# Activation stores of chunks 2 to 5 moved from SyncE's queue to ScalarE's queue in a retention layer followed by a SiLU feed-forward layer

## The chip, the core and the metric

The kernel runs on one core of a Trainium2 chip. The metric is device time in microseconds (us); lower is better. TensorE (PE) multiplies matrices, VectorE (DVE) and ScalarE (ACT) work on tiles element by element, GpSimd (POOL) helps, and SyncE (SP) only issues DMA transfers. In the profile, "PEld" is TensorE's loading of weights, and "SPq" or "ACTq" marks an instruction of an engine's sequencer, such as the issue of a transfer.

## The reference

```python
# q, k, v: (B=4, H=8, S=768, D=64); w_in: (512, 2048); w_out: (2048, 512)
gamma = 1.0 - 2.0 ** (-5.0 - np.arange(H))
for t in range(S):
    state = gamma[None, :, None, None] * state + np.einsum('bhd,bhe->bhde', k[:, :, t], v[:, :, t])
    y[:, :, t] = scale * np.einsum('bhd,bhde->bhe', q[:, :, t], state)
x = y.transpose(0, 2, 1, 3).reshape(B * S, H * D)      # (3072, 512)
h = x @ w_in
g = h * (1.0 / (1.0 + np.exp(-h)))
out = g @ w_out                                        # (3072, 512)
```

The inputs are float32, and every large product is made of three products of split operands.

## The kernel before

**Tiling.** The sequence is cut into NC = 6 chunks of 128 positions. A *unit* is one chunk of one batch, 24 units numbered chunk by chunk. The attention of a unit is spread over three consecutive *visits* (`visit`, `halves`, L606 to L656): transposition of k and q, scores and chunk sums, and then the output y, which is split into three parts `xt` for the next product.

**The first product.** For each chunk c and each of NF = 16 slices f of w_in's columns, `product_in(c, f)` (L659) makes twelve 128x512 matmuls: eight into a PSUM bank `ha` and four into a bank `hb`. Three banks rotate over all ha and hb (`turn`, L376), so a bank is used again by the next product's hb (for an ha) or by the ha of the product after that (for an hb). `close_steps` (L674) then empties them: ACT copies ha to a tile `hs` (L676), DVE subtracts hb (L681), and ACT applies SiLU in place (L686). The result is called g. The pool of `hs` has three buffers (L90).

**The stores in question.** `put_g(keep)` (L689) stores all but the last `keep` of the finished g tiles to a DRAM tile `g_dram` of 256 KB, one per (c, f), by a transfer that SP issues (L692). In the main loop it is called after each product with keep = 1. An `hs` buffer is free again when its store has landed. The name of the last store is kept in `stored`.

**The second product** (`w_out`, `split`, L716 to L737, and the loops from L985 on) starts when all 96 first products are done. It loads the g tiles again (`get`, L698), splits each into three parts on ACT and DVE (L731, L733, L734), and multiplies them with the split w_out. Its outputs are stored by ACT (L1026), but for the last chunk's.

**What sets the order.** PE's order is that of the program. Up to the first visits of chunk 2 the other engines' order is written out by hand too (`early_order`). After that the framework's scheduler orders ACT, DVE, POOL and SP by readiness and program order, within the edges that the kernel draws: `tc.issue_after(x)` puts the instructions of its block behind x on x's own engine, without a wait for x's result.

**SP's other work in the main loop.** From unit 14 on, k and q are transposed by transfers: POOL parts them into 16-bit planes (`part_t`, L415), SP issues two transposing transfers (`turn_t`, L428, issued at L431, whose last is kept in `turned_by`), and ACT joins the planes (`join_t`, L438). SP also loads k, q and v (L164), raw slices of w_in and w_out (`load_w`, L188 for w_out), and stores converted slices (`store_w`, L288). While chunks 3 and 4 are multiplied (`patient`), the raw slices to load are held in `waiting`. In the last six visits the loop (L957 to L968) places SP's work as follows: the two transposes; k and q of the next unit behind them; one product later, v of the next unit behind the latest store of a g; another product later, the waiting raw slices behind the latest store of a g.

During chunk 5's products ACT and DVE also split the w_out slices (L120, L123, L126, L128), which SP loads again (`get_w`, L713).

**Order of the products.** The loop over `steps` runs 92 products: six pairs with chunks 0 and 1, then chunk 2 mixed in for f = 0 to 7, the rest of chunks 0 and 1, chunk 2 for f = 8 to 15, and then chunks 3, 4 and 5. Four products of chunk 0 and 1 come before it. 64 of the 96 products belong to chunks 2 to 5. `LATE` is 2 (L591).

Of the kernel before, what the change touches and what calls it, by code (L numbers as in the profile page):

```python
# [33 lines left out]
def kernel(  # L34
# [28 lines left out]
    nc = tc.nc  # L63
# [17 lines left out]
    def pool(name, bufs, **kw):  # L81
# [14 lines left out]
    g_dram = {(c, f): dram.tile([128, NT], FP32, tag=f"g{c}_{f}", name=f"gd_{c}_{f}")  # L96
              for c in range(NC) for f in range(NF)}
# [48 lines left out]
    def load(name, n):  # L146
        if n >= len(units):
            return
        c, b = units[n]
        src = {"k": k, "q": q, "v": v}[name]  # L150
        if n == 4 * B and name == "k":
            t = conv.tile([128, H, D], FP32, tag="wl", name=f"kf_{n}")
            nc.sync.dma_start(out=t, in_=src[b, :, ds(c * C, C)].rearrange("h t d -> t h d"))
            kqv[name][n] = t
            return
        if n < EARLY:

            if n not in early:
                early[n] = wpool.tile([128, 3, H, D], FP32, tag=f"w{4 + n}", name=f"kqv_{n}")
            t = early[n][:, "kqv".index(name)]  # L160
        else:
            t = ld.tile([128, H, D], FP32, tag=f"{name}f", name=f"{name}f_{n}",
                        bufs=2 if name == "q" else 3)
        nc.sync.dma_start(out=t, in_=src[b, :, ds(c * C, C)].rearrange("h t d -> t h d"))  # L164
        kqv[name][n] = t
# [6 lines left out]
    def load_w(i):  # L172
        if i >= 2 * NF:
            return
        if wide:
            t = stage.tile([128, 2 * DM], U32, tag="wf", name=f"wf_{i}")
            w_in, w_out, n = moe_w_in.bitcast(U32), moe_w_out.bitcast(U32), 256
        else:
            t = stage.tile([128, DM], FP32, tag="wf", name=f"wf_{i}")
            w_in, w_out, n = moe_w_in, moe_w_out, 128  # L180
        if i < NF:
            to = t.rearrange("p (i o f) -> o p i f", o=2, f=n)
            src = w_in[:, ts(i, n)].rearrange("(i o p) f -> o p i f", o=2, p=128)
            nc.sync.dma_start(out=to[0], in_=src[0])
            for j in range(2):
                nc.sync.dma_start(out=to[1, ts(j, D)], in_=src[1, ts(1 - j, D)])
        else:
            nc.sync.dma_start(out=t, in_=w_out[ts(i - NF, 128), :])  # L188
        staged[i] = t
# [71 lines left out]
    def take_w(after=None, parts=False):  # L261

        i = taken[0]
        taken[0] += 1
        if i >= 2 * NF:
            return
        with queue(after) if after else ExitStack():
            rounded = convert_w(i)

        def finish():  # L270
            w32 = rounded()
            if i < NF:
                list(split_w(i, w32, "wi", scale, w_sb))
            else:
                to_store.append((i - NF, w32))

        if parts:
            behind_next.append(finish)
        else:
            with queue(after) if after else ExitStack():  # L280
                finish()
# [3 lines left out]
    def store_w():  # L285
        while to_store:
            f, w32 = to_store.pop(0)
            nc.sync.dma_start(out=wo_dram[f], in_=w32)  # L288
# [101 lines left out]
    def scale_k(n):  # L390
        if 0 <= n < len(units):
            t = kqv["k"][n]
            if units[n][0] == NC - 1:
                t = t[:D]
            if 2 * B + 1 < n < 3 * B + 2:

                def half(heads):
                    for h in heads:
                        nc.scalar.activation(out=t[:, h, :], in_=t[:, h, :], func=AF.Copy,
                                             scale=gk[:, units[n][0], h : h + 1])  # L400

                half(range(H // 2))
                behind_copy.append(lambda: half(range(H // 2, H)))
                return
            g = gk[: t.shape[0], units[n][0], :].unsqueeze(2).to_broadcast([t.shape[0], H, D])
            nc.vector.tensor_tensor(out=t, in0=t, in1=g, op=ALU.mult)
# [6 lines left out]
    planes, turned, turned_by, waiting = {}, {}, [], []  # L413

    def part_t(n, after=None):  # L415

        for name, (p, tag, bufs) in (("q", (ld, "kf", 3)), ("k", (one, "kt", 2))):
            src = kqv[name].pop(n) if name == "q" else kqv[name][n]
            t = p.tile([128, 2 * H * D], U16, tag=tag, name=f"{name}p_{n}", bufs=bufs)
            i = nc.gpsimd.tensor_copy(  # L420
                out=t.rearrange("p (w h d) -> p w h d", w=2, h=H),
                in_=src.bitcast(U16).rearrange("p h (d w) -> p w h d", w=2)).ins
            if after is not None:
                tc.add_manual_dep(i, after.name, mybir.DependencyInfo(
                    mybir.DependencyClass.Sync, mybir.DependencyReason.DATA), reason="later")
            planes[name, n] = t

    def turn_t(n):  # L428
        for name, (p, tag, bufs) in (("q", (ld, "qf", 2)), ("k", (one, "qt", 3))):
            t = p.tile([128, 2 * HP, C], U16, tag=tag, name=f"{name}w_{n}", bufs=bufs)  # L430
            turned_by[:] = [nc.sync.dma_start_transpose(out=t, in_=planes.pop((name, n))).ins]  # L431
            turned[name, n] = t

    def join_t(name, n):

        to, bufs = (qt, 3) if name == "q" else (kt, 2)
        to[n] = one.tile([128, HP, C], FP32, tag=f"{name}t", name=f"{name}t_{n}", bufs=bufs)
        nc.scalar.copy(out=to[n].bitcast(U16).rearrange("p a (t w) -> p w a t", w=2),  # L438
                       in_=turned.pop((name, n)).rearrange("p (w a) t -> p w a t", w=2))
# [151 lines left out]
    LATE = 2  # L591
# [65 lines left out]
    pending, stored = [], []  # L657

    def product_in(c, f):  # L659
        close_in(c, f, *multiply(c, f))  # L660
# [28 lines left out]
    def put_g(keep):  # L689
        while len(pending) > keep:  # L690
            c, f, g = pending.pop(0)
            stored[:] = [nc.sync.dma_start(out=g_dram[c, f], in_=g).ins]  # L692


    order = [(c, f) for c in range(NC) for f in range(NF)]
# [12 lines left out]
    def get_w(f):  # L708
        if f < NF:
            tag = "kqkqq"[f % 5]  # L710
            t = one.tile([128, DM], FP32, tag=f"{tag}t", name=f"wr_{f}",
                         bufs=2 if tag == "k" else 3)
            nc.sync.dma_start(out=t, in_=wo_dram[f])  # L713
            w_got[f] = t

    def w_out(f):  # L716
        list(split_w(f, w_got.pop(f), "wo", 1.0, wo))
        get_w(f + W_READ)
# [117 lines left out]
    SC(4)  # L836
    CL(0), CL(0), CL(0)
    put_g(0)
    W(1)
    T(5)  # L840
# [23 lines left out]
    W(2)  # L864
    CL(1)
    put_g(0)
    T(7)
    P(2)
# [74 lines left out]
    for n, (c, f) in enumerate(steps):  # L943
        if n in scales_at:
            behind_next.append(lambda m=scales_at[n]: scale_k(m))
        if n in joins_at:
            behind_copy.insert(0, lambda m=joins_at[n]: [join_t(name, m) for name in "qk"])
        if n in parts:
            behind_next.append(lambda m=parts[n]: part_t(m, taken_out[0]))
        patient[0] = steps.index((3, 0)) <= n < max(turns_at) + 2  # L950
        product_in(c, f)
        put_g(1)
        store_w()
        if (c, f) in takes:
            take_w(taken_out[0], n < len(pairs + three))
        behind.get((c, f), lambda: None)()
        if n in turns_at:  # L957
            turn_t(turns_at[n])
            if turns_at[n] >= LATER:
                with tc.issue_after(turned_by[0]):  # L960
                    load("k", turns_at[n] + 1), load("q", turns_at[n] + 1)
        if turns_at.get(n - 1, 0) >= LATER:
            with tc.issue_after(stored[0]):
                load("v", turns_at[n - 1] + 1)
        if turns_at.get(n - 2, 0) >= LATER:
            with tc.issue_after(stored[0]):
                while waiting:
                    load_w(waiting.pop(0))  # L968
        for name, m in loads_at.get(n, ()):
            load(name, m)  # L970
        if c == NC - 1:
            if f == 0:
                for i in range(W_READ):
                    get_w(i)
            if f < NF - 4:
                w_out(f)
            if f >= NF - 6:
                if f == NF - 6:
                    for n in range(G_AHEAD):
                        get(n)  # L980
                if f >= NF - S_AHEAD:
                    split(f - NF + S_AHEAD)
# [84 lines left out]
```

## Time and profile before

| What | Value |
|---|---|
| Median of 3 runs (lowest, highest) | 622.12 us (618.11, 622.21) |
| The profiled execution's own time | 620.76 us |
| Its span | 618.9 us, granted TensorE clock 0.999 |
| ACT, SiLU of g (L686) | x96, 627 ns each |
| ACT, copy of ha (L676) | x96, 591 ns each |
| DVE, subtraction of hb (L681) | x96, 683 ns each |
| Stores of g, SP (L692) | x96, 256 KB each, 3.4 us to landing (median) |
| Stores of the output, ACT (L1026) | x20, 256 KB each, 2.1 us to landing (median) |
| Transposing transfers, SP (L431) | x20, 4.2 and 4.5 us to landing (medians) |
| DMA queue q1 (SP's transfers) | 102.79 MB, 59.7% of 16 engines' span |
| DMA queue q10 (ACT's transfers) | 5.24 MB, 2.3% |

The page of a profile gives each engine's busy time and share of the span; a timeline lists instructions by start and duration, with the idle time before one and what ended it in brackets; a list of waits names the waiting line, what it waited for, and total, count and longest in us. The mean of a stage's DMA share is the busy share of the core's 16 DMA engines.

### The profile page before, as it was taken

To read this page: it belongs to the slowest core of one execution; us is meant where nothing else is said; L and a number is where in the kernel's file an instruction comes from. 1 tells how busy PE (TensorE), PEld (TensorE's weight loads), DVE (VectorE), ACT (ScalarE), POOL (GpSimd) and SP (SyncE) were. 2 spreads that over 40 slices of the span, in tenths; PEclk is the share of its full clock that TensorE was granted. 3 is DMA by queue.
4 is the path that set the end of the run, shared out by engine and by line. 5 is a ranking of instruction groups with operands and counts; after the bars stand their busy time and mean duration, and the time that the engine had idled before them with its cause. 6 is when DMAs were issued, how large, how long until landed. Compare 5 with 4: busy or idle time off the path is not lost.

```text
span 618.9 us, 13462 instructions
## 1 busy us (share of the span) xinstructions
PE 601.6 (97%) x5360; PEld 494.6 (80%) x5360; DVE 424.6 (69%) x731; ACT 315.7 (51%) x595; POOL 29.1 (5%) x85
## 2 busy tenths in 40 slices
PE   6898999999999999999999999999999999999997
PEld 5777787888778888887788888888888888888886
DVE  4998889889977777785699783645635453654631
ACT  6677896676667567665588642312221221412311
POOL 3000000100031111120000000000000000000000
PEclk9999999999999999999999999999999999999999
DMA  9998874784789699999777552533524433442301
GB/s 193 221 227 208 220 216 158 202 241 169 250 217 222 184 265 241 275 233 292 273 227 257 193 147 68 169 104 92 180 70 132 140 102 103 141 132 89 116 1 68
DMA packets 144334, 108.88 MB, mean 176 GB/s; under 512 B 101136, under 2 KB 109584, under 8 KB 144272
## 3 DMA queue, kind: packets, MB, share of 16 engines
q1 hardware_dynamic: 141392, 102.79, 59.7%
q10 hardware_dynamic: 2880, 5.24, 2.3%
q8 instruction: 42, 0.69, 0.5%
q14 instruction: 20, 0.16, 0.1%
HBM read 66.06 MB, written 36.70 MB: 166 GB/s over the span
## 4 chain that ended last, share of the span: by engine, by line
PE 73%; DVE 5%; DMA 2%; ACT 2%; issue 1%; SPq 1%; DVEq 0%; POOLq 0%; ACTq 0%
PE o L1007 21%; PE ha L666 18%; PE oa L1007 14%; PE hb L666 10%; PE ob L1007 7%; PE y L513 2%; DMA gd<-g 1%; DVE g L681 1%; DMA yr<-yd 1%; SPq L431 1%; PE sc L474 1%; PE sc L464 1%; DVE ca L218 1%; DVE xt L572 0%; ACT g L676 0%
## 5 line engine op out<-in xcount | busy, mean ns | idle before, releaser
L666 PE MATMUL ha<-xt,wi 128*128 128x512 f32 x768 | 193.7, 394 | 1.3 <-ACT xt L569 0.7
L666 PEld LDWEIGHTS ha<-xt,wi 128*128 128x128 f32 x768 | 141.8, 188 | 33.5 <-ACT xt L569 1.1
L1007 PE MATMUL o<-wo,gs 128*128 128x512 f32 x564 | 143.2, 389 | 0.0
L733 DVE TENSOR_TENSOR gs<-gr,gs 128x512 fp32r<-128x512 f32 x96 | 62.1, 685 | 90.3 <-ACT gs L731 90.3
L1007 PEld LDWEIGHTS o<-wo,gs 128*128 128x128 f32 x564 | 105.9, 188 | 21.9
L731 ACT ACTIVATE gs<-gr 128x512 fp32r<-128x512 f32 x96 | 53.6, 621 | 134.2 <-issue 131.9
L1007 PE MATMUL oa<-wo,gs 128*128 128x512 f32 x376 | 115.8, 389 | 0.0
L666 PE MATMUL hb<-xt,wi 128*128 128x512 f32 x384 | 103.2, 390 | 1.9 <-ACT g L676 0.9
L681 DVE TENSOR_TENSOR g<-g,hb 128x512 f32<-128x512 f32 x96 | 65.6, 683 | 37.1 <-ACT g L676 24.7
L666 PEld LDWEIGHTS hb<-xt,wi 128*128 128x128 f32 x384 | 71.8, 188 | 18.4 <-ACT g L676 1.8
L686 ACT ACTIVATE g<-g 128x512 f32<-128x512 f32 x96 | 60.1, 627 | 46.2 <-DVE g L681 46.2
L1007 PEld LDWEIGHTS oa<-wo,gs 128*128 128x128 f32 x376 | 70.6, 188 | 14.7
L1007 PE MATMUL ob<-wo,gs 128*128 128x512 f32 x188 | 73.7, 392 | 0.0
L676 ACT ACTIVATE g<-ha 128x512 f32<-128x512 f32 x96 | 56.7, 591 | 28.5 <-PE ha L666 11.9
L734 DVE SCALAR_TENSOR_TENSOR gs<-gs 128x512 fp32r<-128x512 f32 x96 | 62.0, 683 | 0.0
L1007 PEld LDWEIGHTS ob<-wo,gs 128*128 128x128 f32 x188 | 35.3, 188 | 8.7 <-DVE o L1025 1.6
L202 ACT ACTIVATE ca<-wf 128x512 f32<-128x512 f32 x32 | 21.4, 668 | 8.0 <-DVE cw L223 5.0
L218 DVE SCALAR_TENSOR_TENSOR ca<-wf,ca 128x512 f32<-128x512 uint32 x32 | 22.7, 710 | 0.5
L1024 ACT ACTIVATE o<-o 128x512 f32<-128x512 f32 x10 | 6.0, 598 | 33.4 <-PE o L1007 33.0
L482 DVE TENSOR_TENSOR am<-sc,decay 128x512 f32<-128x512 f32 x24 | 16.5, 688 | 9.1 <-PE sc L474 9.0
L212 DVE SCALAR_TENSOR_TENSOR cs<-ca,cs 128x512 uint32<-128x512 uint32 x32 | 22.1, 691 | 0.9
L513 PE MATMUL y<-qt,mid 64*64 64x64 f32 x384 | 20.2, 224 | 1.8 <-POOL token L385 1.8
(93 smaller groups left out, 568.4 us busy)
## 6 DMA issues: line engine op xcount, KB each, us to landing
gd<-g SPq DMA_DIRECT2D x96, 256.0 KB, 3.4
gr<-gd SPq DMA_DIRECT2D x96, 256.0 KB, 2.7
wf<-in_moe_w_out_dram SPq DMA_DIRECT2D x16, 512.0 KB, 5.0
out_dram<-o ACTq DMA_DIRECT2D x20, 256.0 KB, 2.1
wf<-in_moe_w_in_dram SPq DMA_DIRECT2D x16, 256.0 KB, 4.2
wf<-in_moe_w_in_dram SPq DMA_DIRECT2D x32, 128.0 KB, 4.0
kf<-in_k_dram SPq DMA_DIRECT2D x16, 256.0 KB, 4.3
qf<-in_q_dram SPq DMA_DIRECT2D x16, 256.0 KB, 4.1
```

Source lines behind the costliest of these rows:

```text
L202: nc.scalar.activation(out=a.bitcast(FP32), in_=hi.bitcast(FP32), func=AF.Abs, scale=65536.0)
L212: nc.vector.scalar_tensor_tensor(out=s, in0=a, scalar=3, in1=s, op0=ALU.logical_shift_left, op1=ALU.bitwise_or)
L218: nc.vector.scalar_tensor_tensor(out=p.bitcast(FP32), in0=lo, scalar=2.0 ** -52, in1=p.bitcast(FP32), op0=ALU.mult, op1=ALU.mult)
L513: i = nc.tensor.matmul(yp[ts(e, D), o, a, :], lhsT=lhsT, rhs=rhs, start=(e, o) not in started, stop=True, skip_group_check=True).ins
L666: nc.tensor.matmul(hb if i == 2 else ha, lhsT=w_sb[f][:, i, ts(kk, 128)], rhs=xt[c][:, i, kk, :], start=kk == 0 and i != 1, stop=kk == KIN ...
L676: copied[:] = [nc.scalar.activation(out=hs, in_=ha, func=AF.Copy, scale=ONE_E).ins]
L681: taken_out[:] = [nc.vector.tensor_tensor(out=hs, in0=hs, in1=hb, op=ALU.subtract).ins]
L686: nc.scalar.activation(out=hs, in_=hs, func=AF.Silu)
L731: nc.scalar.activation(out=t[:, 0, :], in_=g, func=AF.Copy, scale=HALF)
L733: nc.vector.tensor_tensor(out=t[:, 1, :], in0=g, in1=high, op=ALU.subtract)
L734: nc.vector.scalar_tensor_tensor(out=t[:, 2, :], in0=t[:, 1, :].bitcast(FP32), scalar=-1.0 / EPS, in1=high, op0=ALU.mult, op1=ALU.add)
L1007: nc.tensor.matmul(o, lhsT=g, rhs=wo[f][:, i, :], start=f == 0 and i != 1, stop=f == NF - 1 and i != 0)
```

## The change

Stores of g of chunks 2 to 5 (64 of 96) are issued by ACT on its own queue instead of by SP. `stored` is then set only by stores of chunks 0 and 1. The two blocks that put v and the raw slices behind the latest store put them behind the latest transposing transfer instead.

```diff
     def put_g(keep):
         while len(pending) > keep:
             c, f, g = pending.pop(0)
-            stored[:] = [nc.sync.dma_start(out=g_dram[c, f], in_=g).ins]
+            ring = nc.scalar if c >= LATE else nc.sync
+            i = ring.dma_start(out=g_dram[c, f], in_=g).ins
+            if c < LATE:
+                stored[:] = [i]
...
         if turns_at.get(n - 1, 0) >= LATER:
-            with tc.issue_after(stored[0]):
+            with tc.issue_after(turned_by[0]):
                 load("v", turns_at[n - 1] + 1)
         if turns_at.get(n - 2, 0) >= LATER:
-            with tc.issue_after(stored[0]):
+            with tc.issue_after(turned_by[0]):
                 while waiting:
                     load_w(waiting.pop(0))
```

## The prediction

> **What bounds the kernel now.** I read the page first, then busy time by stage, then what TensorE (PE) waited for, then SP's and ACT's instructions around the longest of these waits.
>
> ```profile
> PE 601.6 (97%) x5360; PEld 494.6 (80%) x5360; DVE 424.6 (69%) x731; ACT 315.7 (51%) x595; POOL 29.1 (5%) x85
> ```
>
> PE is busy for 601.6 of 618.9 us, so every stall together is 17.3 us. The change can act only from chunk 2's first product on. Counting steps of 2.72 us (one product, 12 matmuls, in the chain of work) back from the second stage's start at 353.0, and about 2 us for each attention visit, the products of chunk 2 lie at about 110 to 132 us (8 of them) and from 176 us on (56 more, with chunks 3 to 5). Busy time by stage there (columns PE, PEld, DVE, ACT, POOL, clock, DMA share, GB/s):
>
> ```profile
> 98.00:180.00 82.00, 81.16 (x473) 66.10 (x472) 73.22 (x128) 54.94 (x96) 4.59 (x5) 1.00 0.68 208
> 180.00:280.00 100.00, 99.93 (x1456) 82.71 (x1456) 78.07 (x135) 64.91 (x100) 18.24 (x25) 1.00 0.98 238
> 280.00:300.00 20.00, 19.13 (x187) 15.55 (x186) 13.50 (x25) 11.53 (x20) 0.09 (x1) 1.00 0.92 265
> 300.00:320.00 20.00, 19.70 (x146) 16.07 (x145) 15.64 (x28) 14.43 (x26) 0.09 (x1) 1.00 0.78 264
> 320.00:345.00 25.00, 25.00 (x112) 20.49 (x111) 24.84 (x46) 21.02 (x40) 0.00 (x0) 1.00 0.72 245
> ```
>
> PE's idle time is 0.84 + 0.07 + 0.87 + 0.30 = 2.08 us in the whole region: that is the ceiling of any gain, 0.3% of the time. The last row matters for the loss: DVE is at 24.84 of 25 us there, and ACT has 3.98 us to spare. What PE waited for from 176 to 356 us:
>
> ```profile
> PE hb L666 <- ACT g L676: 0.9, 1, 0.9
> PE y L513 <- POOL token L385: 0.3, 1, 0.3
> PE hb L666 <- DVE xt L575: 0.2, 1, 0.2
> ```
>
> Only the first is a matter of stores. Its cause shows on SP and then on ACT:
>
> ```profile
> 278.98 1.28 SPq L431 DMA_TRANSPOSE qw<-qp  x1
> 280.35 2.80 SPq L431 DMA_TRANSPOSE kw<-kp  x1
> 283.25 1.96 SPq L705 DMA_DIRECT2D gr<-gd  x4
> 285.30 0.85 SPq L692 DMA_DIRECT2D gd<-g  x2
> ```
>
> ```profile
> 287.21 0.64 ACT L686 ACTIVATE g<-g 128x512 f32<-128x512 f32 x1
> 292.11 0.60 ACT L676 ACTIVATE g<-ha 128x512 f32<-128x512 f32 x1 [4.26 <-DMA gd<-g]
> ```
>
> A SiLU ended at 281.12, but its store was issued at 285.30, behind two transposing transfers and four loads, and took 6.70 us to land (the chain of work). The three hs buffers were full, the copy out of ha waited 4.26 us, and the bank came free 0.87 us late for PE. The SP queue's own waits show that this is rare and that SP mostly waits for the work:
>
> ```profile
> SPq L692 <- ACT g L686: 48.6, 29, 3.7
> ...
> SPq L692 <- DMA gr<-gd: 1.3, 2, 1.1
> ```
>
> The second line is a store held by an older, unrelated load. That wait would stand on ACT too.
>
> **What the Trainium skill says.** "DMA: Bandwidth & Descriptors", section "Queues, rings and completion order": SP and ACT each own one ring on each of the same 16 DMA engines, without engines or a descriptor generator of their own, and an engine takes turns between the rings packet by packet. So a store on ACT's ring need not follow SP's loads, but shares the engines with them. The trace has SP's rings at 59.7% and ACT's at 2.3%, never both full, so it neither confirms nor denies it. The same page, "Issuing engines are not separate DMA queues": a second issuing engine saves issue time only. With a DMA share of 0.98 from 180 to 280 us I expect the landing (median 4.1 us there) to shorten by less than the queueing. "ScalarE: Activation LUTs", section "What ACT_TABLE_LOAD costs": back-to-back ACTIVATEs overlap by about 93 ns. The trace agrees: 0.62 us activations start 0.52 us apart (323.20, 323.72), an overlap of 0.10, which a store between them forfeits.
>
> **The change part by part.**
>
> *64 stores leave SP* (8 early, 56 after 176 us). SP is not on PE's path except at 292 us. There the store would be issued at about 281.5 instead of 285.3; even 6.7 us of landing then ends before 288.3, and the next stores likewise precede the loads. Gain 0.87 us; between 0 (landing lengthens as much) and 2.08 (everything PE waited for). I take 0.87.
>
> *64 stores join ACT.* The row of an ACT store is 0.338 us of issue (out, x20, at most 0.377). What it costs ACT depends on its place:
>
> ```profile
> 398.03 1.14 ACT L731 ACTIVATE gs<-gr 128x512 fp32r<-128x512 f32 x2
> 398.89 0.34 ACTq L1026 DMA_DIRECT2D out_dram<-o  x1
> 399.27 1.16 ACT L731 ACTIVATE gs<-gr 128x512 fp32r<-128x512 f32 x2
> ```
>
> Here the issue ran while the second activation still did: a third would have begun at 398.03 + 2 x 0.52 = 399.07 and began at 399.27, 0.20 us. A store right behind its own SiLU must wait for its end: 0.63 + 0.02 (semaphore) + 0.34 + about 0.07 of gaps = 1.06 to the next start instead of 0.52, 0.54 us. So 0.20 to 0.54 each; I take the upper end, since the scheduler sees the store ready when the SiLU is done and little else is.
>
> By stage: 180 to 280 us, 64.91 + 30 x 0.54 = 81.1 of 100; 280 to 300, 11.53 + 6 x 0.54 = 14.8 of 20; 300 to 320, 14.43 + 7 x 0.54 = 18.2 of 20; 320 to 345, 21.02 + 9 x 0.54 = 25.9 of 25 (22.8 at 0.20). Behind a store on ACT stand the copy out of ha, for which hb of the next product waits, and the halves of the weight split, for which DVE waits. From the times of ACT and PE, most copies end 1.87 us before the matmul that takes their bank (40 of some 55 at 1.5 or more), so one store of 0.54 is hidden by that cover. Cover is gone at two places: the copy ending at 268.02 (matmul at 268.08) and the one at 292.71, which the gain removes. At the first, ACT had idled 2.11 us before its queue moved, so the store may sit in that hole: 0 to 0.54, I take 0.27.
>
> From 320 to 345 us cover is DVE's:
>
> ```profile
> 324.65 0.68 DVE L681 TENSOR_TENSOR g<-g,hb 128x512 f32<-128x512 f32 x1
> ```
>
> It ends at 325.33, and the matmuls that reuse its bank start near 325.6: about 0.2 us of cover, and 0.15 to 0.5 at seven such subtractions. DVE has no idle time to make up a loss. Its inputs lie 1.0 to 1.9 us ahead at these, but 0.35 to 0.44 us ahead at every third (copy ends 325.50, subtraction at 325.85). A store of 0.54 there costs DVE 0.54 - 0.38 = 0.16 to 0.19; four times is 0.75, less 0.15 of cover: 0.6 us, from 0 (at 0.20 a store) to 1.5 (ACT over by 0.9 as well). After 345 us both engines have room.
>
> *v and raw slices behind the transposes instead of behind a store.* These are five v loads and the slices held back while chunks 3 and 4 run. The same loads on the same queue, each now earlier by a store (0.96 us at 256.00). They still wait for their buffers (slices for DVE up to 2.3 us) with wod stores and the next transposes behind, and visits are some 13 us apart: 0. Without that cover a late transpose would cost the 0.29 us that ACT once waited for qw.
>
> Sum: -0.87 + 0.27 + 0.6 = 0.0. Against the profiled execution (span 618.9, time 620.76) that is 620.8. The median of the runs shown is 1.36 above it, so I say 622.1.
>
> **Rivals.**
>
> *ACT's issue waits behind SP's transposes (the other side, slower).* SP is held 1.24 to 3.44 us in each transpose, a pair at the medians 2.6 us, nine pairs after 176 us, and a step is 2.72 us, so about one store meets each pair. If it must wait out the pair, ACT stands 2.6 + 0.54 = 3.2 us against a cover of 1.87: 1.3 x 9 = 11.7 us. If only the transpose under way, about 0.65 + 0.54 = 1.2: nothing. It decides from 1.9 us of hold. Half of the pairs gives +6: 628. For it: SP stores beside these transposes took up to 1.69 us of issue (median 0.46 from 180 to 280 us), and the skill's shared generator; the older-load wait adds to it. Against: ACT's 20 issues never exceed 0.377, though in a stage without transposes.
>
> *ACT and DVE become the bound from 320 to 345 us.* 0.9 of ACT and up to 1.5 passed on through DVE, with no gain elsewhere: +2.4, 624.5. For: the two fullest rows. Against: the weight halves have slack until the second stage.
>
> *All stalls go and the stores are hidden.* -2.08: 620.0. Against: 1.2 of it has other waits' names.
>
> *The landing gets no shorter* (engines at 0.92 to 0.98). The 0.87 stays: 623.0.
>
> **How the numbers follow.** Forecast 0.50, range 620 to 624 by the bounds and the runs' scatter (618.1 to 622.2); transposes 0.16; ACT and DVE 0.12; all gain 0.12; no shorter landing 0.10. About 1% (6.2 us) is what a measurement of this kernel can tell from no change. Faster than 615.9 would need three times the ceiling: 0.02. Slower than 628.3: most of the transposes' case, 0.12, and 0.02 of ACT's: 0.14. The rest, 0.84, is the same. The range 618.5 to 628.0 leaves out 0.06 below and about 0.14 above.
>
> **What would show it.** Right: gd issues under ACT of about 0.34 us, the 4.26 us wait of a copy for gd gone, ACT near 16 us per 20 before 320 us, PE still full in every row. Wrong: gd issues on ACT of over 1 us beside the transposes, PE waiting for ACT's copies at several visits, or DVE idle with PE from 320 to 345 us.

## The result and the profile after

The changed kernel takes 625.59 us (median of 8 runs, 623.81 to 628.05) against 621.85 us for the kernel before (8 runs, 618.11 to 622.69): a ratio of 1.0077, 95% interval 1.0053 to 1.0100. So it is slower by 0.5 to 1.0%, where 622.1 us was forecast. Its profiled execution took 626.54 us, with a span of 624.8 us. One run of all those below (633.01 us, of the repeated change) was in a slower state of the chip and is left out of the numbers.

Below, "a product" is numbered 0 to 95 in TensorE's (PE's) order. Its time is the start of its last hb matmul. Lines behind the store have moved by three: the store is now L693, `get` L708, the splits of g L734 to L737.

Busy time by stage of the kernel after (columns as before: PE, PEld, DVE, ACT, POOL, clock, DMA share, GB/s):

```profile
98.00:180.00 82.00, 80.63 (x472) 66.00 (x471) 72.41 (x130) 53.80 (x96) 4.13 (x5) 1.00 0.70 209
180.00:280.00 100.00, 98.48 (x1409) 80.75 (x1411) 78.36 (x133) 65.77 (x99) 17.06 (x24) 1.00 1.04 232
280.00:300.00 20.00, 20.00 (x239) 16.57 (x233) 13.45 (x24) 13.51 (x23) 2.06 (x3) 1.00 1.07 293
300.00:320.00 20.00, 19.70 (x146) 16.08 (x145) 15.02 (x27) 12.53 (x22) 0.09 (x1) 1.00 0.70 244
320.00:345.00 25.00, 23.64 (x101) 17.97 (x99) 25.00 (x47) 20.22 (x38) 0.00 (x0) 1.00 0.81 258
```

The row from 280 to 300 us is now full, as forecast. PE's losses are elsewhere: 1.52 us from 180 to 280, where it had been busy for 99.93, and 1.36 us in the last row, where it had never been idle. DVE is at 25.00 of 25 us there. What PE waited for from 176 to 360 us:

```profile
PE hb L666 <- ACT g L676: 1.5, 1, 1.5
PE ha L666 <- DVE g L681: 1.4, 2, 0.7
```

The same products in the two profiled executions, by how much later they are after the change than before:

| Stretch (product) | Later by | Where |
|---|---|---|
| up to 0 | +2.65 us | before 31 us, ahead of every moved instruction |
| 0 to 38 | -0.53 | 31 to 168 us |
| 38 to 47 | +0.15 | |
| 47 to 50 | +1.84 | product 48, before at 205.60 us |
| 66 to 77 | -1.01 | of it -0.94 at product 74, before at 293.56 us: the stall of 292 us |
| 84 to 95 | +2.73 | 322 to 353 us |

The first 2.65 us are scatter between executions: at product 0 the profiles of the other versions stand from 0.85 earlier to 2.39 later. From product 38 on the sum is +3.74 us. One execution of each carries that table; the experiments below say which rows return.

**The stall at product 48.** ACT in the kernel after:

```profile
206.49 1.34 ACT L438 COPY kt<-kw 128x1024 uint16<-128x1024 uint16 x1 [0.95 <-DMA kw<-kp]
207.69 0.62 ACT L686 ACTIVATE g<-g 128x512 f32<-128x512 f32 x1
208.22 0.58 ACT L676 ACTIVATE g<-ha 128x512 f32<-128x512 f32 x1
208.34 0.33 ACTq L693 DMA_DIRECT2D gd<-g  x1
```

The copy out of ha at 208.22 is the one that was at 203.81 before:

```profile
203.81 0.60 ACT L676 ACTIVATE g<-ha 128x512 f32<-128x512 f32 x1
```

It is 4.41 us later, of which 2.3 us is the lag that PE already had. Most of the rest are two waits of ACT for transposing transfers. The copy stood behind the joining of k's planes (206.49), which waited 0.95 us, and ACT had already lost 0.82 us to the q transfer before it:

```profile
195.67 1.38 ACT L438 COPY qt<-qw 128x1024 uint16<-128x1024 uint16 x1 [0.82 <-DMA qw<-qp]
```

SP and POOL show why the transfers were late. After the change:

```profile
188.55 3.25 SPq L431 DMA_TRANSPOSE qw<-qp  x1
191.91 1.39 SPq L431 DMA_TRANSPOSE kw<-kp  x1
...
196.83 1.24 SPq L431 DMA_TRANSPOSE qw<-qp  x1
...
199.47 3.01 SPq L431 DMA_TRANSPOSE kw<-kp  x1
```

and before:

```profile
186.22 1.24 SPq L431 DMA_TRANSPOSE qw<-qp  x1
...
195.18 1.24 SPq L431 DMA_TRANSPOSE kw<-kp  x1
```

POOL after the change:

```profile
195.76 1.04 POOL L420 COPY qp<-qf 128x1024 uint16<-128x1024 uint16 x1 [4.50 <-DMA qw<-qp]
```

The first q transfer took 3.25 us to issue and 7.1 us to land (before: 1.24 and 3.3). POOL could not part the next q until it had landed, so the next q transfer was issued at 196.83 instead of 190.79, and the k transfer behind it took another 3.01 us to issue and 6.9 to land (1.24 and 5.0). The issue of the moved store, at 208.34, takes 0.33 us and holds up neither the SiLU nor the copy, which began before it.

**The stall at 292 us** is gone: the copy there no longer names gd.

```profile
291.79 1.36 ACT L438 COPY kt<-kw 128x1024 uint16<-128x1024 uint16 x1 [1.55 <-DMA kw<-kp]
293.01 0.62 ACT L686 ACTIVATE g<-g 128x512 f32<-128x512 f32 x1
293.54 0.57 ACT L676 ACTIVATE g<-ha 128x512 f32<-128x512 f32 x1
```

**From 320 to 345 us** VectorE's order has changed. Between the subtractions of products 85 and 86 the kernel before has seven other instructions, in 4.02 us:

```profile
325.85 0.68 DVE L681 TENSOR_TENSOR g<-g,hb 128x512 f32<-128x512 f32 x1
...
329.87 0.68 DVE L681 TENSOR_TENSOR g<-g,hb 128x512 f32<-128x512 f32 x1
```

Between the same two subtractions the kernel after has nine, in 5.21 us. The two more are splits of a g for the second product, 0.60 us each:

```profile
329.59 0.69 DVE L681 TENSOR_TENSOR g<-g,hb 128x512 f32<-128x512 f32 x1
...
331.12 0.69 DVE L737 SCALAR_TENSOR_TENSOR gs<-gs 128x512 fp32r<-128x512 f32 x1
331.72 0.69 DVE L736 TENSOR_TENSOR gs<-gr,gs 128x512 fp32r<-128x512 f32 x1
...
334.80 0.70 DVE L681 TENSOR_TENSOR g<-g,hb 128x512 f32<-128x512 f32 x1
```

Counted over chunk 5, the first eight of DVE's split instructions stand behind 80, 81, 82, 82, 92, 93, 93 and 93 subtractions before, and behind 80, 81, 81, 82, 82, 86, 86 and 89 after. Four have moved forward by 4 to 10 products, and 4 x 0.60 = 2.4 us of work has come in front of the subtractions of products 82 to 89, where DVE had no idle time.

### The profile page after: what moved, and what is told of

Same layout as the page of the kernel before. It is cut to its first block, busy times and chain, and to the rows that moved or that the text cites. A ratio compares the mean times of both kernels' runs of the same rounds, so it can differ in the third digit from the quotient of the medians.

```text
span 624.8 us, 13444 instructions
## 1 busy us (share of the span) xinstructions
PE 603.9 (97%) x5360; PEld 494.8 (79%) x5360; DVE 424.6 (68%) x731; ACT 317.7 (51%) x595; POOL 29.3 (5%) x85
## 4 chain that ended last, share of the span: by engine, by line
PE 79%; DVE 2%; DMA 1%; issue 1%; ACT 0%; SPq 0%; DVEq 0%; POOLq 0%; ACTq 0%
PE ha L666 23%; PE o L1010 20%; PE oa L1010 14%; PE hb L666 11%; PE ob L1010 7%; PE y L513 2%; DMA kw<-kp 1%; PE sc L474 1%; PE sc L464 1%; DVE g L681 0%; PE o L1018 0%; DVE wol L123 0%; PE oa L1018 0%; DVE wo L128 0%; DVE cs L212 0%
## 5 line engine op out<-in xcount | busy, mean ns | idle before, releaser
L666 PE MATMUL ha<-xt,wi 128*128 128x512 f32 x768 | 195.7, 397 | 3.1 <-DVE g L681 2.4
L734 ACT ACTIVATE gs<-gr 128x512 fp32r<-128x512 f32 x96 | 53.6, 621 | 134.2 <-issue 131.8
L737 DVE SCALAR_TENSOR_TENSOR gs<-gs 128x512 fp32r<-128x512 f32 x96 | 62.2, 686 | 0.0
```

The costliest lines, as they stand in the source:

```text
L666: nc.tensor.matmul(hb if i == 2 else ha, lhsT=w_sb[f][:, i, ts(kk, 128)], rhs=xt[c][:, i, kk, :], start=kk == 0 and i != 1, stop=kk == KIN ...
L734: nc.scalar.activation(out=t[:, 0, :], in_=g, func=AF.Copy, scale=HALF)
L737: nc.vector.scalar_tensor_tensor(out=t[:, 2, :], in0=t[:, 1, :].bitcast(FP32), scalar=-1.0 / EPS, in1=high, op0=ALU.mult, op1=ALU.add)
```

## The experiments

All are edits of the changed kernel, if nothing else is said, so v and the raw slices stand behind the transposing transfers in them too. Each was timed beside the kernel before on the same chip. "Stretch" numbers are products, as in the table, against the profile before.

**1. Which chunk's stores cost?** Chunks 2 to 4, chunk 5, or none:

```diff
-            ring = nc.scalar if c >= LATE else nc.sync
+            ring = nc.scalar if LATE <= c < NC - 1 else nc.sync    # chunks 2 to 4
+            ring = nc.scalar if c == NC - 1 else nc.sync           # chunk 5
+            ring = nc.sync                                         # order of v and slices only
```

> Stores of chunks 2 to 4 on ACT, those of chunk 5 back on SP. Theory (two separate losses: transposing transfers that land late beside ACT's stores near 205 us, worth +1.8 us; and the scheduler moving the splits of the second product's first g tiles forward into DVE's full stretch, worth +2.7 us, which chunk 5's stores cause; with a gain of 0.9 us at 292 us): about +0.9 us against the kernel before, no stall between 320 and 350 us. Rival (ACT's issue time itself is the cost, spread over all 64 stores): 48 of 64 of the +3.8 us, +2.8 us, with DVE idle waiting for ACT's copies.

> Only chunk 5's 16 stores on ACT. Theory: +2.7 us against the kernel before from stalls of PE for the subtraction between 320 and 350 us, and the 0.9 us stall at 292 us stays. Rival (issue time of each store): 16 of 64 of +3.8 us, +0.9 us.

> All stores on SP as before; only v and the raw slices are ordered behind the transposing transfers. Theory: 0, within 0.5 us of the kernel before. Rival (the loads placed earlier crowd the transposing transfers): +1 to +2 us with the stall near 205 us.

| Version | Median (range, runs) | Before | Ratio, 95% | 47-50 | 66-77 | 84-95 |
|---|---|---|---|---|---|---|
| chunks 2 to 4 | 624.76 (621.69-628.39, 15) | 621.55 | 1.0062 (1.0038-1.0086) | 0.00 | +0.99 | -0.02 |
| chunk 5 | 624.78 (623.73-626.47, 8) | 621.55 | 1.0063 (1.0042-1.0085) | 0.00 | -0.26 | +2.87 |
| order only | 622.79 (620.73-625.65, 21) | 621.55 | 1.0015 (0.9996-1.0034) | 0.00 | +0.42 | -0.01 |

The loss behind product 84 belongs to chunk 5's stores. Chunks 2 to 4 cost more than expected. Their profile shows no stall at product 48, but one of 1.35 us at product 73; its execution (623.47 us) lies below its median. At product 73 the copy waited for a store: the one that ACT issued at 279.56, right behind its SiLU, took 9.58 us to land.

```profile
289.22 0.60 ACT L676 ACTIVATE g<-ha 128x512 f32<-128x512 f32 x1 [2.95 <-DMA gd<-g]
```

Placing v and the slices behind the transposes ("order only") costs nothing that these runs can tell from zero, though up to 0.34% lies within the interval. DVE, ACT and POOL keep their order there; on SP four loads of v, from 216 to 258 us, have each passed one store. Where the stores stay on SP this has an effect. Product 67 comes 0.44 to 1.17 us later in all five profiles with the loads of v moved and the stores of chunks 3 and 4 on SP (0.45 in "order only", 0.59 in "chunk 5"), and some 6 us earlier a copy waited 0.5 to 1.1 us for a store. Neither stands in any other profile.

**2. Is it the early splits?** The splits were held behind the latest subtraction and copy, first in the changed kernel, then in the kernel before:

```diff
-                    split(f - NF + S_AHEAD)
+                    with queue(taken_out[0]), queue(copied[0]):
+                        split(f - NF + S_AHEAD)
```

> The changed kernel, with the first three splits of g for the second product held behind the copies and subtractions of chunk 5's last three products. Theory: the 2.7 us between 320 and 350 us go, +1.0 us against the kernel before remains. Rival (stores on ACT delay the inputs of DVE there): the stalls stay, +3.8 us.

> The kernel before, with the first three splits of g held behind chunk 5's last three products. Theory: the kernel before has no stall there and the splits stood late already: within 0.6 us of the kernel before. Rival (holding reorders DVE for the worse, as it may have done in the run with both): +1 to +2 us with stalls between 330 and 350 us.

The changed kernel took 626.94 us (625.62 to 629.17, 6 runs), ratio 1.0099 (1.0072 to 1.0125); the expected recovery did not come. The splits did move back (six of the eight stand behind 94 to 96 subtractions), but +1.72 us from 84 to 95 stayed. The rest of the order had changed again. DVE itself now waited for ACT, 0.91 us at the largest loss:

```profile
331.01 0.43 DVE L208 TENSOR_SCALAR ca<-ca 128x512 f32<-128x512 f32 x1 [0.91 <-ACT ca L202]
```

ACT's instruction stood behind a SiLU that waited for DVE's last subtraction, and PE then waited 1.03 us for the next one. This is the late input of DVE that the rival named; no store stood in ACT's chain from that subtraction to this input. The kernel before with the same hold took 621.48 us (14 runs), ratio 0.9990 (0.9964 to 1.0015). So holding does no harm by itself, but it does not restore the order before. The reverse was cleaner: the kernel before, every store on SP, with the splits written earlier in the program:

```diff
-    S_AHEAD = 3
+    S_AHEAD = 4
...
-            if f >= NF - 6:
-                if f == NF - 6:
-                    for n in range(G_AHEAD):
-                        get(n)
-                if f >= NF - S_AHEAD:
-                    split(f - NF + S_AHEAD)
+            if f == 2:
+                for n in range(G_AHEAD):
+                    get(n)
+            if f in (4, 5, 6, 7):
+                split(f - 4)
```

> The kernel before, all stores on SP; only the loads and splits of the second product's first four g tiles are called earlier, in chunk 5's products 4 to 7, so that they stand in DVE's order before the subtractions of products 7 and 8 rather than of 12 and 13. Theory (order alone: four more DVE operations of 0.60 us in a stretch where DVE has no time to spare): PE waits for subtractions between 320 and 350 us, +2 to +2.9 us against the kernel before. Rival (the stores' time on ACT, or inputs of DVE that they delay, makes those stalls): within 0.5 us of the kernel before.

It took 624.30 us (22 runs), ratio 1.0043 (1.0027 to 1.0059), with +2.41 us from 84 to 95. Its row and its wait from 320 to 345 us are nearly those of the changed kernel:

```profile
320.00:345.00 25.00, 23.70 (x101) 18.36 (x100) 25.00 (x46) 19.47 (x35) 0.00 (x0) 1.00 0.72 235
```

```profile
PE ha L666 <- DVE g L681: 1.3, 3, 0.6
```

Its splits stand behind 87, 88, 88 and 88 subtractions where the kernel before has 92, 93, 93 and 93. So early splits, with the loads on SP and the first parts on ACT that belong to them, are enough for this loss; no store on ACT is needed.

**3. What do chunks 2 to 4 cost?** First the bytes: the version "chunks 2 to 4" with stores of half a tile.

```diff
-            ring = nc.scalar if c >= LATE else nc.sync
-            i = ring.dma_start(out=g_dram[c, f], in_=g).ins
+            ring = nc.scalar if LATE <= c < NC - 1 else nc.sync
+            cols = ts(0, NT // 2) if LATE <= c < NC - 1 else ts(0, NT)
+            i = ring.dma_start(out=g_dram[c, f][:, cols], in_=g[:, cols]).ins
...
-        nc.sync.dma_start(out=g, in_=g_dram[c, f])
+        for j in range(2):
+            cols = ts(0 if LATE <= c < NC - 1 else j, NT // 2)
+            nc.sync.dma_start(out=g[:, ts(j, NT // 2)], in_=g_dram[c, f][:, cols])
```

> As the run with chunks 2 to 4 on ACT, but these 48 stores move only half of each tile (the left 256 columns; the other half is not stored, and the later load reads the left half twice). ACT issues as many stores. Theory (two rings competing for the DMA engines make the transposing transfers land late): transposes land at about 4.5 us in the median instead of 5.5, loads of q, k and v at about 4.2 instead of 5.2, and the loss of some 3 us shrinks to under 1 us. Rival (the issue on ACT or the changed order costs it): landings may shorten, but +3 us against the kernel before stays.

It took 621.64 us (14 runs), ratio 0.9997 (0.9973 to 1.0021): no cost. I took that for proof of a shortage of transfer bandwidth, and it is not one, for the halved stores also left DVE's order between 100 and 177 us as before, where that of "chunks 2 to 4" differs (below). Then other parts:

```diff
-            ring = nc.scalar if c >= LATE else nc.sync
+            ring = nc.scalar if c in (3, 4) else nc.sync
+            ring = nc.scalar if c == LATE and f >= NF // 2 else nc.sync
+            ring = nc.scalar if c > LATE else nc.sync
+            ring = nc.scalar if c == LATE else nc.sync
```

> Only the stores of chunks 3 and 4 on ACT, those of chunks 2 and 5 on SP. Theory: the visits of chunk 2's second half lie closest together (one per two products), so most of the transposes' loss goes with chunk 2: +0.5 to +1.5 us against the kernel before, transposes from 216 us on landing as late as in the changed kernel. Rival (every chunk loses alike): two thirds of +3.2 us, +2.1 us.

> Only the 8 stores of chunk 2's second half (f from 8 on, the products with a visit after every second one) on ACT, all others on SP. Theory: this is where two rings make the transposing transfers too late, because four visits follow each other closely; nearly the whole loss of the run with chunks 2 to 4 on ACT (+3.2 us) comes back, +2 to +3 us. Rival (the loss needs many stores on ACT): 8 of 48, +0.5 us.

> The changed kernel with chunk 2's 16 stores back on SP. Theory: the stalls for the subtractions between 320 and 350 us stay (+2.7 us), no stall near 205 us, the stall at 292 us goes: +1.8 to +2.9 us against the kernel before, some 1 to 2 us below the changed kernel. Rival (chunk 2 doesn't matter): as the changed kernel.

> Only the sixteen stores of chunk 2 are issued by ScalarE; those of chunks 3 to 5 stay on SyncE's queue, v and raw slices stay behind the transposes. Theory (chunk 2's stores lengthen the landings of the transposing transfers between 176 and 210 us, and when two long landings follow each other, ScalarE's joins and the copy behind them come late): landings of about 5 to 7 us there instead of 3.3 to 5.0, a stall of TensorE of 0.2 to 2.2 us at the products 47 to 50, nothing from 320 us on; median 0.6 to 1.9 us over before, since the whole change minus the version without chunk 2 gave 1.6 us in the last batch. Rival (chunk 2's stores cost only together with those of chunks 3 and 4): no stall at 47 to 50, median within 0.5 us of before. Rival (the second half of chunk 2 is enough, the early eight cost nothing): the same median as for the second half alone, 0.9 us over before, within 0.5.

The changed kernel was run again beside the second and third of these:

> The changed kernel again, on the same chip and beside the same runs of the kernel before as the other two: +3.8 us if the losses of the parts don't depend on each other's runs, and not over +5 us, since the two parts alone (+3.2 and +3.2 us) would then have to overlap.

| Version | Median (range, runs) | Before | Ratio, 95% | 38-50 | 66-77 | 84-95 |
|---|---|---|---|---|---|---|
| chunks 3, 4 | 622.47 (619.2-623.77, 14) | 621.96 | 0.9999 (0.9978-1.0020) | -0.01 | -1.22 | +0.02 |
| chunk 2, last eight | 623.03 (620.8-628.47, 14) | 622.16 | 1.0009 (0.9984-1.0035) | +0.21 | +0.61 | +0.02 |
| chunks 3 to 5 | 624.67 (621.81-628.5, 20) | 622.16 | 1.0039 (1.0023-1.0055) | -0.01 | -1.21 | +2.73 |
| chunk 2 | 625.25 (620.71-629.64, 22) | 621.98 | 1.0046 (1.0025-1.0067) | +2.90 | +0.45 | -0.01 |
| the change again | 626.11 (623.45-630.01, 14) | 622.16 | 1.0075 (1.0052-1.0098) | +3.27 | -1.06 | +2.73 |

Within their intervals chunk 2 and chunks 3 to 5 add up: 0.46% + 0.39% = 0.85%, against 0.75% for the whole. Chunks 3 and 4 show no cost, and chunk 2's last eight none clear of zero, although I had expected both to cost. Chunk 2 cost more than expected (2.9 us, not 0.6 to 1.9). So what costs in chunk 2 is its first eight stores, at 103 to 133 us, or these together with the last eight. Of the +0.45 of "chunk 2" from 66 to 77, +1.17 are at product 67, where the whole change loses nothing.

**4. Order or competition?** Comparing the orders of the engines in all profiles, a different order of DVE, ACT and SP between 100 and 177 us stands in just those versions that move chunk 2's first eight stores whole (with the halved stores ACT and SP differ at 123 to 127 us only, and DVE not at all). Among other things a load of v is issued behind a load of k: in "chunk 2" at 176.70 us instead of 172.55. Last pair:

```diff
+            ring = nc.scalar if c == LATE and f < NF // 2 else nc.sync    # first eight
+            ring = nc.scalar if (c, f) >= (LATE, NF // 2) else nc.sync    # all but these
```

> Only the first eight stores of chunk 2, at about 110 to 132 us, are issued by ScalarE; every later one stays on SyncE's queue. Theory (the first eight stores make the scheduler order VectorE, ScalarE and SyncE differently between 125 and 177 us, a v load is issued behind a k load and 2 to 4 us later, and what follows comes late): VectorE's order there as in the changed kernel, a stall of TensorE of 1 to 3 us between the products 38 and 50, median 2 to 3 us over before. Rival (the later stores on ScalarE's queue compete with the transposing transfers): no ScalarE store from 176 us on, so landings there as before (3.3 to 5.0 us), no stall at product 48, median within 0.7 us of before. Both needed: landings as before, a little stall, median 0.5 to 1.5 us over.

> All stores of the change but the first eight of chunk 2 are issued by ScalarE. Theory (the order from 125 to 177 us costs): order there as before, no stall at product 48 beyond 0.3 us, the 0.9 us at 292 us gained and the 2.7 us from 320 us on lost; median as with chunks 3 to 5, about 2.4 us over before (1.6 to 3.0), some 1.5 us under the whole change. Rival (the competition from 176 us on costs): a stall of about 1.8 us at product 48, median 3.5 to 4.5 us over before.

The first eight alone: 624.80 us (619.55 to 628.10, 22 runs) against 621.87, ratio 1.0038 (1.0016 to 1.0060). All but these: 625.31 us (621.40 to 630.14, 22 runs), ratio 1.0052 (1.0032 to 1.0072). With the first eight alone no store of a g is on ACT's queue after 133 us, and the kernel still loses. So these eight, with the moved loads of v, cost something without the later stores. "All but these" lies between its two forecasts (3.2 us in the ratio, against 2.4 and 3.5 to 4.5): it has the +2.73 from product 84, no stall at 48, and +0.84 at 73, again behind a copy that waited 2.40 us for a store on ACT. What PE waited for longest with the first eight alone, from 100 to 360 us:

```profile
PE hb L666 <- ACT g L676: 1.9, 2, 1.1
PE ha L666 <- DVE g L681: 1.1, 1, 1.1
```

The 1.1 us of the first line is at product 67, not at 48. There "order only", "chunk 5" and "chunk 2, last eight", with the order before, lost 0.44 to 0.59 us too, so at most the rest can be put down to the order before 177 us. The second line is at product 39 (0.3 us in the kernel before), and all but 0.17 us of it was made up by product 40; the same +0.8 and -0.6 are in all six profiles with this order. So this one profile does not show where the order costs. That the cost is the order's rather than that of eight stores on ACT is argued: each of their issues took at most 0.36 us, and with the halved stores as many, in DVE's old order, cost nothing.

A stall at product 48 of 1.67 to 2.25 us is in four profiles (the change, its repetition, "splits held", "chunk 2"), all of which have both the changed order and ACT's stores from 176 us on; of the versions that have only one of the two, none shows more than 0.20 there. "Chunks 2 to 4" has both and does not show it.

Both conditions show in the landings of the transposing transfers (and one waits for the other through POOL, as above). From 176 to 216 us (lowest, median, highest), in "chunks 3 to 5", with the order before and these stores on SP:

```profile
DMA to landing us min/median/max: 3.2/3.8/5.1
```

in "all but these", with the order before and the stores on ACT, and in "first eight", with the changed order and the stores on SP:

```profile
DMA to landing us min/median/max: 3.3/4.1/6.8
DMA to landing us min/median/max: 3.3/4.6/5.7
```

and in "chunk 2", with the changed order and the stores on ACT:

```profile
DMA to landing us min/median/max: 3.6/5.8/6.9
```

Whether the two together cost more time than each alone the medians do not show: 0.38% (first eight) and 0.09% (last eight) make up the 0.46% of chunk 2. That the longest landings on SP's queue are longer beside stores of ACT (6.8 and 6.9 against 5.1 and 5.7 us) fits the Trainium skill, "DMA: Bandwidth & Descriptors", section "Queues, rings and completion order", by which an engine takes turns between the rings packet by packet.

## Why the prediction failed

- **PE bounds the kernel, and its stalls before are a ceiling on the gain: right.** No version was measurably faster than the kernel before.
- **The stall at 292 us, -0.87: its size was one execution's.** It measured -0.94. But product 74 also came 0.75 to 1.15 us earlier in versions that keep those stores on SP ("chunk 5" -0.88, "order only" -0.75, "splits early" -1.15), where the copy still waited for the store, though less (1.38 us in "splits early", 2.70 in "order only", against 4.26). And stores on ACT could land late too: in "chunks 2 to 4" and "all but these" the copy waited 2.95 and 2.40 us for one. So a gain of this size through the move is not shown.
- **An issue on ACT, 0.20 to 0.54 us each, under the copies' cover: no loss is seen from it.** The store on ACT took 0.326 us (median of 30 from 176 to 285 us, highest 1.63), and with 32 of them "chunks 3, 4" lost nothing. The term of +0.27 at 268 us did not come (-0.06 at product 67).
- **Rival "ACT's issue waits behind SP's transposes": did not come.** ACT was hardly held. SP's own issues grew from 176 to 285 us: the median of its k transfers from 1.36 to 2.38 us, that of its v loads from 0.42 to 1.20. The v loads' new place in SP's queue alone gives up to 1.68 (last section), and the k transfers' median is 1.32 in "chunks 3, 4" with 32 stores on ACT. That either grew because of ACT's stores is not shown.
- **"The same loads on the same queue, each now earlier by a store": 0 in the time, as far as can be told.** "Order only" is that step alone. What the step left out is its other side, that each store on SP then stands later by a load of v (product 67, above); the changed kernel, with the stores on ACT, lost nothing there.
- **The landing of the other transfers: no term.** That of the transposes went from 4.5 to 5.4 us (median, 176 to 285 us), that of the q, k and v loads from 4.0 to 5.6. The skill's sharing of engines was quoted, but used only on the stores' landing, not on the transposes'. For a late transpose the prediction had 0.29 us without cover; at product 48 it was 1.8 in the profiled execution.
- **+0.6 from 320 to 345 us: the failed term of the sum.** It measured +2.73. The full row of DVE and its cover of 0.2 us were read rightly. The step that failed is its mechanism: it let DVE's order stand and made its inputs late by a store's issue on ACT. In fact the scheduler, which orders all engines but PE, was given a program in which chunk 5's stores sit elsewhere, and it put four splits of 0.60 us into the full stretch. The rival of ACT and DVE had this place and nearly this size (2.4), but ACT was not over (20.22 of 25 us), and "splits early" lost nearly as much with no store on ACT. DVE was not idle there, as the prediction's sign of being wrong had it, but full.
- **Chunk 2's eight early stores: no term at all.** The prediction counted them ("8 early") and priced nothing between 110 and 176 us. Alone they cost 0.38% (0.16 to 0.60), about 2.4 us, the moved loads of v included.

The sum was 0.0. What was measured is about 0.4% for chunk 5's stores, which the order of the splits explains, and a part for chunk 2's early stores. As an estimate, the latter is 0.23% (first eight 0.38 less "order only" 0.15) or 0.24% (the change, 0.76 in the mean of its two measurements, less "all but these" 0.52), about 1.5 us; neither difference is clear of noise by itself.

Its cause stays open. In the profiles of the change itself the loss is the stall at product 48 and goes with late transposing transfers. The profile of "first eight" has no such stall; of its 1.28 us behind product 38, 1.07 are at product 67, where the change itself loses nothing, and the rest of its loss is mixed with the scatter at the start. And the order between 100 and 177 us was never imposed with all stores on SP, so it was not tried without early stores on ACT.

## What to carry to other kernels

Where a scheduler orders the engines, moving an instruction to another queue is two changes: the move itself, and whatever new order the scheduler makes of everything else; price the second by comparing orders, first in the stretches where an engine has no idle time. Ask too what a store taken off a busy queue does to the landing of the transfers left there, when others wait for them: the transposing ones took up to 6.8 us beside the moved stores where they had taken up to 5.0 (176 to 216 us, "all but these" and before). And a row of full busy time says where an engine has no room, which is where four instructions of 0.6 us cost more than all the gain that 64 moved stores could have brought (2.7 us against at most 2.08).

## What the hardware showed beside that

- **How long an issue takes depends on what stands before it in its queue.** In "order only", with all stores on SP, the four loads of v right behind a load of q took 0.93 to 1.68 us to issue, and the others, behind a store, 0.39 to 0.43. In the kernel before it was the store between them that took longer (0.96 us at 256.00). So a longer issue on SP is no sign by itself of traffic on ACT's queue.
- **The moved stores landed no sooner.** From 176 to 285 us ACT's stores landed in 4.6 us (median), those of SP before in 4.1. From 176 to 290 us the DMA share rose from 0.98 to 1.05 while the rate fell from 239 to 234 GB/s.
- **PE's busy time understates a stall.** From 320 to 345 us it fell by 1.36 us. The matmul records fell from 112 to 101, which at 2.72 / 12 = 0.227 us each is 2.5 us (some records can be missing), and the products themselves end 2.73 us later.
